# A planner's order changed: first loads, ranks, planned lengths, and one wide exponential in every third attention unit

## The chip, the cores and the metric

The kernel runs on one core of one Trainium2 chip. The metric is the time of one execution on the device in microseconds (us). The engines are TensorE (PE; its weight loads are listed as PEld), VectorE (DVE), ScalarE (ACT), GpSimd (POOL) and SyncE (SP), which only issues the transfers (DMAs) here.

## The reference

Banded attention feeds a gated feed-forward block with a spatial mixing. There are 8 batches, 8 heads, 576 positions and 64 features a head, all in float32 (w_in and w_out arrive as float64).

```python
scores = scale * np.matmul(q, k.transpose(0, 1, 3, 2))
mask_plain = (rel >= 0) & (rel < 32)                           # heads 0..3
mask_dil = (rel >= 0) & (rel < 128) & (rel % 4 == 0)           # heads 4..7
attn = softmax(np.where(masks, scores, -1e9))
x = np.matmul(attn, v)                                         # to (8, 576, 512)
h = np.maximum(x @ w_in, 0.0)                                  # 1024 wide
u, v = h[..., :512], h[..., 512:]
v_n = (v - mean(v)) / np.sqrt(var(v) + 1e-6)                   # over the 512 features
v_s = np.einsum('ts,bsd->btd', w_spatial, v_n) + b_spatial[None, :, None]
out = (u * v_s) @ w_out                                        # (8, 576, 512)
```

## The kernel before

**A planner writes the order.** The kernel is a set of strands, Python generators that yield what they need next (results of other strands, buffers, then an engine with a planned length in us) and emit their instructions when they are served. `Timeline.run` picks, again and again, the strand with the smallest `start + W * rank`: its planned start on its engine plus a small weight W times its rank. So each engine's instruction order, and SP's order of loads, is fixed when the kernel is built. On the chip an engine runs its instructions in that order and waits where an operand is late. The planned lengths steer only the choice; a rank of 1 is worth W us (0.12). `DVE2` and `POOL` share a planned port.

**Precision.** Matmuls with weights or features are made of three passes: each operand is split into a high and a low part (`h`, `l`), and high·high, high·low and low·high are added. The split of a float32 tile is a copy on ACT (line 348, 365, 578, 651 or 781, rounding to the high part) and a difference on DVE (`sub`, line 272) or POOL (`gsub`, line 275).

**Loads.** Everything loaded stands in 12 rotating buffers `kqv`. `heads_in` brings keys and queries of a pair of heads (4 pairs a batch), `values_in` its values, `weight_in` one of 8 chunks of w_in (`halves[half, c]`; half 1 is the value half, half 0 the gate's other factor) or 4 of w_out (`outs`), `spatial_in` one of 5 chunks of the spatial matrix, `bias_in` the bias. The list `first` is the order of the first loads on SP. Once the values of batch 0 and the first half of w_in are there, `reserve` takes nine of the buffers for good: three each for the sums of w_out (`o`), of w_in (`u`) and for `fac`.

**Weights.** `weight` turns a float64 chunk into high and low parts: ACT scales (line 311), DVE does four bit operations (313 to 321), ACT rounds the high part (348), and the low part is made in one of three ways, listed in `ways`: on PE as three matmuls with the identity and a copy by ACT (327 to 331), on DVE as two operations (272, 342), or on POOL. `spatial` splits a float32 chunk (ACT 365, DVE 272); it has a way over PE, which is switched off.

**Attention.** A unit is a third of the positions for two pairs of heads: 6 units a batch (two groups G, three units u each). Scores on PE (461), scale and mask (DVE 480), negated maximum (DVE 482), six exponentials with their sums on ACT (488), a small addition (ACT 491), reciprocal (DVE 501), the product with it on POOL (503), transposes on PE (508), a copy (ACT 511). `weighted` multiplies with the values (PE 536), `evacuated` copies to `raw` (ACT 563), `features_in` splits (ACT 578, DVE 272 and 582).

**Feed-forward.** `v_tile` makes 5 tiles of the value half (PE 605, 619), their rectified copy (ACT 611), statistics (DVE 637 to 639), the root on POOL (641) and the normalised, split tile (DVE 644, ACT 651; low part on POOL in batch 0 and on DVE after). `upper` is the other half for batch 0 (PE 681, ACT 686). From batch 1 on it is made with seven block products instead of eight (Strassen's scheme, `piece` with kind `u`, PE 818), which needs sums of blocks of w_in (`summed`, POOL 734 and 736, DVE, ACT) and factors, sums of feature blocks (`factor`, ACT 781 and DVE 272; `differences`, POOL 808). `gate` is the spatial mixing for a block of features and half of the positions (14 matmuls, PE 698 to 700) and the product with the other half on DVE (705). The output uses the same seven products (kind `o`); each product's result is added on DVE (854) or copied (ACT 856), and finished blocks go out (865). `warm` fills PE with matmuls on zeros (877) for the planned first 30 us.

Batch 1's attention is planned into batch 0's feed-forward, and so on; `AO` and `AS` set the ranks of its units.

Of the kernel before, what the change touches and what calls it, by code (L numbers as in the profile page):

```python
# [25 lines left out]
class Timeline:  # L26
# [71 lines left out]
    def run(self):  # L98
        W = 0.12
        while self.strands:  # L100
# [39 lines left out]
def tile_banded_attention_gated_moe(  # L140
# [24 lines left out]
    B, NPAIR, _, S = kT.shape  # L165
# [10 lines left out]
    US = 3  # L176
    NU = NS // US
# [179 lines left out]
    def spatial(sc):  # L357
        yield [("in", sc)]
        if sc == 4:
            yield [("bias",)]  # L360
        big = staged[sc]
        w = big[1][:, :S]
        yield ACT, 0.575, 0.1
        if sc < 4:
            nc.scalar.copy(wt[0][:, sc, :], w)
            if not (False):
                yield DVE2, 0.75
                sub(wt[1][:, sc, :], w, wt[0][:, sc, :])
            for ts in (slice(0, HS), slice(HS, S)) if False else ():
                yield "bank"  # L370
                (bank,) = yield PE, 0.63
                pl = bank[1][:, :HS]
                nc.tensor.matmul(pl, ident, w[:, ts], start=True, stop=False)
                nc.tensor.matmul(pl, minus, wt[0][:, sc, ts], start=False, stop=True)
                yield ACT, 0.29, 0.11
                nc.scalar.copy(wt[1][:, sc, ts], pl)
                tl.give(bank)
        else:
            nc.scalar.copy(wa, w)
            yield DVE2, 0.75  # L380
            sub(wb[:TAIL], w[:TAIL], wa[:TAIL])
        tl.give(big)
        tl.done("wt", sc)
# [63 lines left out]
    def unit(b, G, u):  # L447
# [34 lines left out]
        nc.vector.tensor_reduce(nm, flat, axis=AX.X, op=ALU.max, negate=True)  # L482
        if True:
            for e in range(US):
                yield ACT, 0.58 + 0.2 * (e == US - 1)
                for j in range(2):
                    i = 2 * e + j
                    nc.scalar.activation(  # L488
                        p[:, e, j], p[:, e, j], AF.Exp, bias=nm[:, i : i + 1], accum_out=sm[:, i : i + 1]
                    )  # L490
            nc.scalar.activation(sm, sm, AF.Copy, bias=1e-9)
            yield DVE, 0.11, 0.085
        else:
            yield POOL, 0.79, 0.04
            nc.gpsimd.tensor_add(flat, flat, nm.unsqueeze(2).broadcast_to([P, 2 * US, KW]))
            yield ACT, 0.425, 0.1
            nc.scalar.activation(p, p, AF.Exp)
            yield DVE, 0.83, 0.085
            nc.vector.reduce_sum(sm, flat, axis=AX.X)
            nc.vector.tensor_scalar_add(sm, sm, 1e-9)  # L500
# [56 lines left out]
    def evacuated(b, hp, h, acc):  # L557
        if hp >= NPAIR // 2:
            dst = raws[b, hp][1].rearrange("p (j r f) -> p f r j", f=2, r=2)[:, h]
        else:  # L560
            dst = raws[b, hp][1].rearrange("p (a r j) -> p a r j", a=2, r=2)[:, h]
        yield ACT, 0.3, 0.24
        nc.scalar.copy(dst, acc[1][1][:, :HS].rearrange("p (r j) -> p r j", r=2))  # L563
# [108 lines left out]
    def upper(b, h, f):  # L672
        fs = slice(f * P, (f + 1) * P)
        ts = slice(h * HS, h * HS + HS)
        yield [("v", b, t) for t in range(4)] + [("wi", 0, c) for c in range(NC)]
        yield "mm bank ur"
# [13 lines left out]
    def gate(b, h, f):  # L690
        fs = slice(f * P, (f + 1) * P)
        ts = slice(h * HS, h * HS + HS)
        yield [("vn", b, t) for t in range(5)] + [("wt", c) for c in range(5)] + [("bias",)]
        yield "mm bank"
        held = yield PE, 1.86
# [103 lines left out]
    def differences(b, kind, i):  # L799
# [5 lines left out]
        for n, need, a, c, to in zip((1, 3, 2, 4), needs, ((1, i), (1, 2 + i), (1, 2 + i), (0, i)), ((0, i), (1, i), (0, i), (0, 2 + i)), ((0, i), (1, i), (0, i), (0, 2 + i))):  # L805
            yield need
            yield POOL, 0.66, 0.04
            nc.gpsimd.tensor_sub(at(*to), at(*a), at(*c))  # L808
# [24 lines left out]
    def piece(b, kind, m, name, left, steps):  # L833

        if kind == "u" and len(name) == 2:
            yield [("v", b, t) for t in range(4)] + [("x", b, c, 0) for c in range(NC)]
        else:
            yield [("fac", b, kind, name)]
        yield [("wo", c) if kind == "o" else ("wi", 0, c) for c in range(NC)] + [("sum", kind, n, i) for n in range(1, 5) for i in range(2)]
        yield "mm bank"  # L840
        held = yield PE, 0.8
# [43 lines left out]

    ways = ((POOL, DVE, PE, DVE), (PE, PE, PE, PE), (PE, PE, DVE, DVE))
    halves = {}
    for half in (1, 0):
        cols = slice(half * NF, half * NF + NF)
        for c in range(NC):  # L890
# [3 lines left out]
            halves[half, c] = weight_in(("wi", half, c), src)  # L894
            r = -0.75 + 0.09 * c if half else -0.44 + 0.09 * c
            tl.add(r, weight(("wi", half, c), wi[0][:, c, cols], wi[1][:, c, cols], w_in.dtype, ways[1 - half][c]))
    outs = [weight_in(("wo", c), (w_out[c * P : c * P + P, 0],)) for c in range(NC)]
    first = [
        heads_in(0, 2), heads_in(0, 1, 0, 1), bias_in(), heads_in(0, 0, 0, 1), halves[1, 0], heads_in(0, 1, 1, NU),
        heads_in(0, 0, 1, NU), heads_in(0, 3), spatial_in(4), halves[1, 1], halves[1, 2], halves[0, 2],  # L900
        halves[0, 0], values_in(0, 0), values_in(0, 1), values_in(0, 2), halves[1, 3], halves[0, 3],
        values_in(0, 3), spatial_in(1), halves[0, 1], outs[2], outs[0], outs[3],
        outs[1], spatial_in(0), spatial_in(3), spatial_in(2),
    ]
    for n, strand in enumerate(first):
        tl.add(2 * n - 200, strand)
    for c in range(NC):
        tl.add(-1.06 + 0 * c, weight(("wo", c), wo[0][:, c, :], wo[1][:, c, :], w_out.dtype, ways[2][c]))
    for c in range(5):
        tl.add(-0.02 if c < 4 else -0.33, spatial(c))  # L910
    tl.add(-0.82, bias())
    for b in range(B):
        AO, AS = (-0.5, 0.4) if b == 1 else (0.1, 0.6)
        for hp in range(NPAIR):
# [11 lines left out]
        for n, (h, f) in enumerate(itertools.product(range(2), (0, 2, 1, 3))):  # L926
            if b < FU:
                tl.add(b + 0.15 + 0.02 * n, upper(b, h, f))
            tl.add(b + 0.3 + 0.05 * n, gate(b, h, f))
        for hp in range(NPAIR):  # L930
            tl.add(b - 1 + -0.25 + 0.01 * hp, features_in(b, hp))
        far = lambda row, col: lambda i: (col, 2 * row + i)
        for n, (name, source) in enumerate(
            (("11", far(0, 0)), ("21", far(1, 0)), ("1", far(0, 0)), ("2", far(0, 0)), ("3", far(0, 1)), ("22", far(1, 1)), ("4", far(1, 0)))
        ):
            tl.add(b + 1.0 + 0.0 * n, factor(b, "o", name, source))
            if b >= FU and len(name) == 1:
                tl.add(b + 0.1 + 0.0 * n, factor(b, "u", name, source))
        for i in range(2):
            tl.add(b + 1.0 + 0.01 * i, differences(b, "o", i))  # L940
            if b >= FU:
                tl.add(b + 0.7 + 0.01 * i, differences(b, "u", i))
        add, less = nc.vector.tensor_add, nc.vector.tensor_sub
        for kind, w_ in (("u", [x[:, :, :DM] for x in wi]), ("o", wo)):
# [9 lines left out]
            for m in range(2):  # L954
                for n, (name, left, steps) in enumerate(order):
                    r = b + (0.85 + 0.04 * n if kind == "o" else 0.3 + 0.02 * n) + 0.01 * m
                    if kind == "o" or b >= FU:
                        tl.add(r, piece(b, kind, m, name, left, steps))
    for n in range(3):
        tl.add(-0.75, reserve("o", n))  # L960
        tl.add(-0.75 + 0.01, reserve("u", n))
    for n in range(3):
        tl.add(-0.1, reserve("fac", n))
    for i in range(2):
        tl.add(0.0, summed("o", i))
        tl.add(0.8, summed("u", i))
    with tc.manual_schedule(engines={ENGINES.PE, ENGINES.Activation, ENGINES.DVE, ENGINES.Pool, ENGINES.SP}):
# [65 lines left out]
```

## Time and profile before

| | |
|---|---|
| median of 3 runs | 556.21 us (554.93 to 556.61) |
| the profiled execution | 554.37 us, its span 552.6 us |
| granted TensorE clock, mean | 0.989 |
| busy: PE, DVE, ACT, POOL | 538.2, 423.5, 331.9, 195.6 us |
| loaded and stored | 56.68 MB, mean 103 GB/s |

A row of a group of instructions reads: line, engine, operation, output<-input, shape, count | busy us, mean ns of one | idle time of the engine just before them, and what ended it. A row of the timeline is: start us, length us, engine, line, operation, count, and in brackets the idle time before it and what released it. A row of the table of stretches is: the stretch, its length, busy us of each engine (with the number of instructions), the granted clock, the busy share of the DMA engines, GB/s. The ends of PE's matmuls are modelled: its pace is read from the starts.

### The profile page before, as it was taken

What the parts mean: (1) busy time and instruction counts of PE and PEld (TensorE: products, weight loads), DVE (VectorE), ACT (ScalarE), POOL (GpSimd) and SP (SyncE); (2) the same over time, 40 slices, a digit from 0 to 9 for tenths busy, and PEclk for the clock granted to TensorE, in tenths of its full rate; (3) what the DMA queues carried; (4) which work ended last, traced back from release to release, by engine and by line L of the source; (5) the groups of instructions that cost most, each with busy time, mean ns of one, the idle gap of its engine ahead of it and who ended that gap; (6) DMA issues with size and microseconds to landing.
All of it is one profiled execution on the core that took longest, in us unless ns stands there. A gap on an engine that the chain in (4) does not pass through costs nothing.

```text
span 552.6 us, 18450 instructions
## 1 busy us (share of the span) xinstructions
PE 538.2 (97%) x7575; PEld 488.6 (88%) x7575; DVE 423.5 (77%) x1010; ACT 331.9 (60%) x1125; POOL 195.6 (35%) x239
## 2 busy tenths in 40 slices
PE   9899979999999999999999999999999999999997
PEld 7677769987899899998999899998999899998997
DVE  5688976899866795868866796868866796868846
ACT  4887688655738556574737556574737556574212
POOL 3310174643416241342416241342416241342231
PEclk9999997999999999999999999999999999999999
DMA  8996571200433414151433414161433414120102
GB/s 254 236 214 258 128 177 47 67 35 34 131 89 90 120 56 125 54 150 57 143 89 89 121 55 121 57 168 41 142 89 89 121 56 119 59 66 11 55 2 86
DMA packets 97449, 56.68 MB, mean 103 GB/s; under 512 B 78290, under 2 KB 87506, under 8 KB 97364
## 3 DMA queue, kind: packets, MB, share of 16 engines
q1 hardware_dynamic: 97364, 55.50, 36.1%
q8 instruction: 59, 0.97, 0.8%
q14 instruction: 26, 0.21, 0.1%
HBM read 46.04 MB, written 9.44 MB: 100 GB/s over the span
## 4 chain that ended last, share of the span: by engine, by line
PE 43%; DVE 25%; POOL 3%; ACT 3%; issue 1%; DVEq 0%; POOLq 0%
PE bank L818 17%; PE bank L698 13%; DVE fac L272 5%; DVE ur L854 4%; PE bank L536 4%; DVE bn L637 3%; PE bank L508 3%; DVE vnl L272 3%; PE bank L461 2%; PE bank L605 2%; ACT raw L563 2%; DVE nm L482 2%; DVE p L480 2%; DVE xl L272 2%; POOL p L503 2%; DVE mid L644 2%
## 5 line engine op out<-in xcount | busy, mean ns | idle before, releaser
L854 DVE TENSOR_TENSOR ur<-ur,bank 128x288 f32<-128x288 f32 x210 | 88.5, 447 | 34.3 <-PE bank L818 33.2
L488 ACT ACTIVATE p<-p,nm 128x64 f32<-128x64 f32 x288 | 96.2, 335 | 3.6 <-DVE nm L482 3.4
L781 ACT CAST fac<-ur 128x288 fp32r<-128x288 f32 x112 | 45.9, 434 | 74.8 <-DVE ur L705 52.9
L698 PE MATMUL bank<-wth,vnh 128*128 128x288 f32 x256 | 77.2, 302 | 0.0
L698 PE MATMUL bank<-wtl,vnh 128*128 128x288 f32 x256 | 75.7, 296 | 0.0
L698 PE MATMUL bank<-wth,vnl 128*128 128x288 f32 x256 | 75.6, 295 | 0.0
L641 POOL TENSOR_TENSOR rs<-rs,halfneg 128x1 f32<-128x1 f32 (+1 forms) x40 | 30.7, 768 | 121.5 <-DVE rs L639 121.5
L808 POOL TENSOR_TENSOR ur<-ur,ur 128x288 f32<-128x288 f32 x64 | 54.5, 856 | 48.9 <-DVE ur L705 39.6
L272 DVE TENSOR_TENSOR fac<-ur,fac 128x288 fp32r<-128x288 f32 x112 | 59.0, 540 | 7.7 <-ACT fac L781 6.9
L503 POOL TENSOR_TENSOR p<-p,rv 128x384 f32<-128x384 f32 x48 | 40.2, 843 | 53.0 <-DVE rv L501 42.0
L818 PE MATMUL bank<-fac,woh 128*128 128x288 f32 x256 | 54.1, 302 | 1.3 <-DVE ur L854 1.3
L488 ACT ACTIVATION_READ_ACCUMULATOR p<-p,nm 128x1 f32 x288 | 53.9, 187 | 0.0
L808 POOL TENSOR_TENSOR raw<-raw,raw 128x288 f32<-128x288 f32 x42 | 37.5, 900 | 46.2 <-DVE fac L272 26.0
L605 PE MATMUL bank<-wih,xl 128*128 128x512 f32 x128 | 50.1, 392 | 0.0
L605 PE MATMUL bank<-wih,xh 128*128 128x512 f32 x128 | 50.0, 391 | 0.0
L605 PE MATMUL bank<-wil,xh 128*128 128x512 f32 x128 | 49.9, 390 | 0.0
L698 PEld LDWEIGHTS bank<-wth,vnh 128*128 128x128 f32 x256 | 48.2, 188 | 0.6
L698 PEld LDWEIGHTS bank<-wtl,vnh 128*128 128x128 f32 x256 | 48.2, 188 | 0.0
L698 PEld LDWEIGHTS bank<-wth,vnl 128*128 128x128 f32 x256 | 48.1, 188 | 0.0
L705 DVE SCALAR_TENSOR_TENSOR ur<-ur,bank 128x288 f32<-128x288 f32 x64 | 28.7, 449 | 24.5 <-PE bank L700 23.7
L818 PE MATMUL bank<-fac,o 128*128 128x288 f32 x288 | 43.2, 298 | 0.0
L818 PEld LDWEIGHTS bank<-fac,woh 128*128 128x128 f32 x256 | 40.9, 189 | 2.3 <-DVE ur L854 1.8
(146 smaller groups left out, 1323.5 us busy)
## 6 DMA issues: line engine op xcount, KB each, us to landing
kqv<-in_vw_dram SPq DMA_DIRECT2D x128, 144.0 KB, 3.5
out_dram<-ur SPq DMA_DIRECT2D x64, 144.0 KB, 1.8
kqv<-in_kT_dram SPq DMA_DIRECT2D x30, 304.0 KB, 4.1
kqv<-in_qT_dram SPq DMA_DIRECT2D x30, 288.0 KB, 4.2
kqv<-in_w_in_dram SPq DMA_DIRECT2D x16, 256.0 KB, 6.4
kqv<-in_w_out_dram SPq DMA_DIRECT2D x4, 512.0 KB, 7.3
kqv<-in_w_spT_dram SPq DMA_DIRECT2D x5, 288.0 KB, 6.6
kqv<-in_kT_dram SPq DMA_DIRECT2D x2, 192.0 KB, 4.4
```

The source lines that it names most:

```text
L272: nc.vector.tensor_sub(out, a, b.bitcast(F32))
L488: nc.scalar.activation(p[:, e, j], p[:, e, j], AF.Exp, bias=nm[:, i : i + 1], accum_out=sm[:, i : i + 1])
L503: nc.gpsimd.tensor_mul(flat, flat, rv.unsqueeze(2).broadcast_to([P, 2 * US, KW]))
L536: nc.tensor.matmul(acc[j][1][1][i * D : i * D + D, (g - h * HB) * QB : (g - h * HB + 1) * QB], v[r, g, :], probs[b, G, u][1][r, e, q * QB ...
L605: nc.tensor.matmul(pm, x[c][a][:, cols], wi[w][:, c, NF:], start=c == 0 and n == 0, stop=c == NC - 1 and n == 2)
L641: nc.gpsimd.tensor_tensor(rs[:m], rs[:m], halfneg[:m], op=ALU.pow)
L698: nc.tensor.matmul(pv, vn[c][a][:, fs], wt[w][:, c, ts], start=n == 0, stop=False)
L705: nc.vector.scalar_tensor_tensor(ur, ur, 0.0, pv, op0=ALU.max, op1=ALU.mult)
L781: nc.scalar.copy(dst[:, 0, i, :], src)
L808: nc.gpsimd.tensor_sub(at(*to), at(*a), at(*c))
L818: nc.tensor.matmul(bank[:, :HS], left(i, w)[:, m * P : m * P + P], right, start=n == 0, stop=n == 5)
L854: op(ob[1], mine[src][1], bank[:, :HS])
```

## The change

Nothing of the arithmetic on batches changes but in the third unit of each group (`u == 2`). There POOL subtracts the maximum from the whole tile, ACT takes one exponential over all 384 columns, and DVE sums it and adds the small constant, in place of six exponentials with sums and ACT's addition. The code for it stood behind `if True` before:

```python
            yield POOL, 0.79, 0.04
            nc.gpsimd.tensor_add(flat, flat, nm.unsqueeze(2).broadcast_to([P, 2 * US, KW]))
            yield ACT, 0.425, 0.1
            nc.scalar.activation(p, p, AF.Exp)
            yield DVE, 0.83, 0.085
            nc.vector.reduce_sum(sm, flat, axis=AX.X)
            nc.vector.tensor_scalar_add(sm, sm, 1e-9)
```

The first loads come in another order, the low parts of weights are made in other ways (nine chunks over PE instead of seven, two over DVE instead of four, one over POOL as before), and two spatial chunks go over PE. The rest are planned lengths, ranks, W, and what a strand waits for in the plan.

```diff
     def run(self):
-        W = 0.12
+        W = 0.05
...
             nc.scalar.copy(wt[0][:, sc, :], w)
-            if not (False):
+            if not (sc in (1, 2,)):
...
                 sub(wt[1][:, sc, :], w, wt[0][:, sc, :])
-            for ts in (slice(0, HS), slice(HS, S)) if False else ():
+            for ts in (slice(0, HS), slice(HS, S)) if sc in (1, 2,) else ():
...
         nc.vector.tensor_reduce(nm, flat, axis=AX.X, op=ALU.max, negate=True)
-        if True:
+        if u < 2:
             for e in range(US):
-                yield ACT, 0.58 + 0.2 * (e == US - 1)
+                yield ACT, 0.664 + 0.115 * (e == US - 1), 0.1 * (e == US - 1)
...
             dst = raws[b, hp][1].rearrange("p (a r j) -> p a r j", a=2, r=2)[:, h]
-        yield ACT, 0.3, 0.24
+        yield ACT, 0.465 if hp >= NPAIR // 2 else 0.3, 0.1
...
         ts = slice(h * HS, h * HS + HS)
-        yield [("v", b, t) for t in range(4)] + [("wi", 0, c) for c in range(NC)]
+        yield [("v", b, t) for t in range(5)] + [("wi", 0, c) for c in range(NC)]
...
         yield [("vn", b, t) for t in range(5)] + [("wt", c) for c in range(5)] + [("bias",)]
+        if b >= FU:
+            yield [("prod", b, "u", (("21", "4"), ("22", "1"))[h][f // 2], f % 2)]
+        else:
+            yield [("used", b, h, f)]
...
             yield need
-            yield POOL, 0.66, 0.04
+            yield POOL, 0.77, 0.04
...
         if kind == "u" and len(name) == 2:
-            yield [("v", b, t) for t in range(4)] + [("x", b, c, 0) for c in range(NC)]
+            yield [("v", b, t) for t in range(5)] + [("x", b, c, 0) for c in range(NC)]
...
             yield [("fac", b, kind, name)]
+        if kind == "u":
+            yield [("made", b - 1, "o", n, "1w") for n in range(2)]
         yield [("wo", c) if kind == "o" else ("wi", 0, c) for c in range(NC)] + [("sum", kind, n, i) for n in range(1, 5) for i in range(2)]
+        chain = ("11", "21", "2", "3", "1", "22")
+        if name != "11":
+            yield [("prod", b, kind, chain[chain.index(name) - 1] if name in chain else "1", m)]
...
 
-    ways = ((POOL, DVE, PE, DVE), (PE, PE, PE, PE), (PE, PE, DVE, DVE))
+    ways = ((POOL, PE, PE, PE), (DVE, PE, PE, PE), (PE, PE, DVE, PE))
...
             halves[half, c] = weight_in(("wi", half, c), src)
-            r = -0.75 + 0.09 * c if half else -0.44 + 0.09 * c
+            r = -2.32 + 0.02 * c if half else -2.91 + 0.2 * c
...
     first = [
-        heads_in(0, 2), heads_in(0, 1, 0, 1), bias_in(), heads_in(0, 0, 0, 1), halves[1, 0], heads_in(0, 1, 1, NU),
-        heads_in(0, 0, 1, NU), heads_in(0, 3), spatial_in(4), halves[1, 1], halves[1, 2], halves[0, 2],
-        halves[0, 0], values_in(0, 0), values_in(0, 1), values_in(0, 2), halves[1, 3], halves[0, 3],
-        values_in(0, 3), spatial_in(1), halves[0, 1], outs[2], outs[0], outs[3],
-        outs[1], spatial_in(0), spatial_in(3), spatial_in(2),
+        halves[0, 0], heads_in(0, 0, 0, 1), heads_in(0, 1, 0, 1), halves[1, 0], heads_in(0, 2), bias_in(),
+        spatial_in(4), heads_in(0, 0, 1, NU), heads_in(0, 1, 1, NU), heads_in(0, 3), values_in(0, 0), halves[0, 3],
+        halves[1, 2], halves[0, 2], halves[1, 3], values_in(0, 1), outs[2], halves[1, 1],
+        values_in(0, 2), values_in(0, 3), spatial_in(1), halves[0, 1], outs[1], spatial_in(3),
+        outs[3], spatial_in(0), spatial_in(2), outs[0],
...
     for c in range(NC):
-        tl.add(-1.06 + 0 * c, weight(("wo", c), wo[0][:, c, :], wo[1][:, c, :], w_out.dtype, ways[2][c]))
+        tl.add(-1.01 + 0.24 * c, weight(("wo", c), wo[0][:, c, :], wo[1][:, c, :], w_out.dtype, ways[2][c]))
     for c in range(5):
-        tl.add(-0.02 if c < 4 else -0.33, spatial(c))
-    tl.add(-0.82, bias())
+        tl.add(0.57 if c < 4 else -1.09, spatial(c))
+    tl.add(-0.74, bias())
     for b in range(B):
-        AO, AS = (-0.5, 0.4) if b == 1 else (0.1, 0.6)
+        AO, AS = (-0.9, 0.7) if b == 1 else (0.1, 0.6)
...
             if b < FU:
-                tl.add(b + 0.15 + 0.02 * n, upper(b, h, f))
-            tl.add(b + 0.3 + 0.05 * n, gate(b, h, f))
+                tl.add(b + -0.6 + 0.06 * n, upper(b, h, f))
+            tl.add(b + 0.75 + 0.0 * n, gate(b, h, f))
         for hp in range(NPAIR):
-            tl.add(b - 1 + -0.25 + 0.01 * hp, features_in(b, hp))
+            tl.add(b - 1 + -0.2 + 0.01 * hp, features_in(b, hp))
...
         ):
-            tl.add(b + 1.0 + 0.0 * n, factor(b, "o", name, source))
+            tl.add(b + 0.95 + 0.0 * n, factor(b, "o", name, source))
             if b >= FU and len(name) == 1:
-                tl.add(b + 0.1 + 0.0 * n, factor(b, "u", name, source))
+                tl.add(b + 0.1 + 0.02 * n, factor(b, "u", name, source))
         for i in range(2):
-            tl.add(b + 1.0 + 0.01 * i, differences(b, "o", i))
+            tl.add(b + 0.95 + 0.01 * i, differences(b, "o", i))
             if b >= FU:
-                tl.add(b + 0.7 + 0.01 * i, differences(b, "u", i))
+                tl.add(b + 0.55 + 0.01 * i, differences(b, "u", i))
...
                 for n, (name, left, steps) in enumerate(order):
-                    r = b + (0.85 + 0.04 * n if kind == "o" else 0.3 + 0.02 * n) + 0.01 * m
+                    r = b + (0.85 + 0.03 * n if kind == "o" else 0.35 + 0.06 * n) + 0.01 * m
...
     for n in range(3):
-        tl.add(-0.75, reserve("o", n))
-        tl.add(-0.75 + 0.01, reserve("u", n))
+        tl.add(-0.7, reserve("o", n))
+        tl.add(-0.7 + 0.01, reserve("u", n))
     for n in range(3):
-        tl.add(-0.1, reserve("fac", n))
+        tl.add(0.95, reserve("fac", n))
     for i in range(2):
-        tl.add(0.0, summed("o", i))
-        tl.add(0.8, summed("u", i))
+        tl.add(0.5, summed("o", i))
+        tl.add(0.6, summed("u", i))
```

## The prediction

> **What bounds the kernel now.** I read the page's busy shares and slices first, since a planner's new order can only pay where the bounding engine has holes.
>
> ```profile
> span 552.6 us, 18450 instructions
> ...
> PE 538.2 (97%) x7575; PEld 488.6 (88%) x7575; DVE 423.5 (77%) x1010; ACT 331.9 (60%) x1125; POOL 195.6 (35%) x239
> ...
> PE   9899979999999999999999999999999999999997
> ...
> PEclk9999997999999999999999999999999999999999
> ```
>
> TensorE (PE) is busy for 97% of the span, and one slice, the seventh, shows a lower granted clock. The next view is the table of stretches, cut where the work changes: loading and first attention, first value tiles, the first batch's feed-forward, one regular batch, and the last batch.
>
> ```profile
> core 0: us, PE busy (x) PEld busy (x) DVE busy (x) ACT busy (x) POOL busy (x), PEclk, DMA share, GB/s
> 0.00:34.00 34.00, 31.21 (x396) 24.20 (x396) 20.97 (x56) 22.07 (x93) 12.21 (x25) 1.00 0.92 238
> 34.00:62.00 28.00, 27.77 (x380) 19.79 (x379) 24.46 (x48) 23.09 (x44) 0.69 (x1) 1.00 0.67 190
> 62.00:76.40 14.40, 13.95 (x229) 12.96 (x227) 13.88 (x33) 8.31 (x28) 6.83 (x7) 1.00 1.00 242
> 76.40:91.00 14.60, 11.24 (x271) 9.53 (x274) 7.65 (x19) 12.78 (x54) 8.17 (x9) 0.65 0.19 43
> 91.00:112.00 21.00, 21.00 (x327) 20.51 (x327) 18.12 (x37) 14.06 (x51) 12.21 (x11) 1.00 0.31 88
> 112.00:130.00 18.00, 18.00 (x132) 15.36 (x133) 17.45 (x46) 10.87 (x26) 8.96 (x10) 1.00 0.05 19
> 130.00:148.00 18.00, 16.36 (x217) 14.46 (x207) 17.00 (x42) 10.71 (x48) 7.36 (x9) 1.00 0.29 84
> ...
> 272.90:335.10 62.20, 61.96 (x932) 57.34 (x930) 47.59 (x117) 38.03 (x136) 22.41 (x29) 1.00 0.34 97
> 491.70:552.60 60.90, 57.24 (x390) 54.56 (x390) 44.69 (x104) 20.75 (x47) 15.70 (x19) 0.99 0.11 38
> ```
>
> A regular batch takes 62.2 us, of which PE idles 0.24: nothing to win there by order, something to lose. The holes lie elsewhere: 14.60 − 11.24 = 3.36 us at 76.4 to 91, where the clock is also 0.65; 1.64 us at 130 to 148, where VectorE (DVE) is busy for 17.00 of 18; and the warm-up time before 34. The hole at 76.4, instruction by instruction on PE:
>
> ```profile
> 76.27 0.29 PE L681 MATMUL bank<-xh,wil 128*128 128x288 f32 x1
> 78.00 0.55 PE L508 MATMUL bank<-plus,p 128*128 128x128 f32 x3 [1.45 <-POOL p L503]
> 79.70 0.55 PE L508 MATMUL bank<-plus,p 128*128 128x128 f32 x3 [1.16 <-POOL p L503]
> 81.00 2.25 PE L536 MATMUL bank<-pT,kqv 64*64 64x32 f32 x72 [0.75 <-ACT pT L511]
> ...
> 88.54 0.44 PE L681 MATMUL bank<-xl,wih 128*128 128x288 f32 x1
> 88.78 0.44 PE L681 MATMUL bank<-xh,wil 128*128 128x288 f32 x1
> ...
> 90.58 0.29 PE L681 MATMUL bank<-xl,wih 128*128 128x288 f32 x1
> 90.71 0.29 PE L681 MATMUL bank<-xh,wil 128*128 128x288 f32 x1
> ```
>
> The three waits sum to 3.36 us. After them equal matmuls start 0.24 us apart (88.54, 88.78) instead of 0.13 (90.58, 90.71): the clock is halved from 81.0 to about 90.4, which wastes half of 9.4 us, 4.7. **The hole costs 3.36 + 4.7 = 8.1 us of PE time.** Here a page speaks: the Trainium skill, "TensorE: Matmul & The Clock Gate", section "Why this matters for your kernels", asks for no PE-idle gaps over about 3 us, one idle window bringing the half clock. No single gap here exceeds 1.45 us, and the clock fell all the same; read gap by gap the rule would price the hole at 3.4 us and bring the forecast out 4.7 us later, about no change. The trace's clock speaks against that reading, so it gets no chance of its own: a cluster of short waits is enough.
>
> Who makes PE wait there is on GpSimd (POOL):
>
> ```profile
> 73.92 1.28 POOL L734 TENSOR_TENSOR mid<-woh,wol 128x512 f32<-128x512 f32 x1
> 75.17 1.29 POOL L736 TENSOR_TENSOR mid<-woh,wol 128x512 f32<-128x512 f32 x1
> ...
> 77.12 0.83 POOL L503 TENSOR_TENSOR p<-p,rv 128x384 f32<-128x384 f32 x1 [0.16 <-DVE rv L501]
> ...
> 81.93 2.50 POOL L275 TENSOR_TENSOR vnl<-mid,vnh 128x512 fp32r<-128x512 f32 x2
> ```
>
> Batch 1's attention and batch 0's normalised value tiles share POOL with the block sums (lines 734, 736), and the last value tile is done only at 84.4, because DVE was full (13.88 of 14.40) before. The gates need it; PE had nothing else left.
>
> **The change, part by part.**
>
> *More passes on PE.* PE finishes 9 weight chunks instead of 7 and two spatial chunks instead of none. Rows for the price, with the warm-up ahead of it:
>
> ```profile
> 24.93 7.55 PE L877 MATMUL bank<-vnl 128*128 128x512 f32 x32
> 32.31 1.06 PE L327 MATMUL bank<-kqv,plus 128*128 128x512 f32 x2
> ...
> 33.68 0.63 PE L877 MATMUL bank<-vnl 128*128 128x512 f32 x2
> ```
>
> One chunk holds PE from 32.31 to 33.68, 1.37 us; two more are 2.74. A spatial half has two of the three products and 288 of 512 columns: between 0.51 (scaled by both) and 0.77 us (by columns alone), taken 0.64, four of them 2.56. Together +5.3 us of PE work. But from 24.93 to 32.3 PE did nothing but 32 warm-up matmuls, and the new load order brings four chunks with a PE finish ahead of the second values load, where before one was finished by 34. Three more of them in warm-up time hide 3 × 1.37 = 4.1. Net **+1.2**; bounds −0.2 (a fourth hides as well) and +5.3 (none does, and the warm-up goes on as now). ScalarE (ACT) gets the extra copies, but loses more, below.
>
> *Less on DVE.* Ways that end on DVE fall from four to two, and two spatial differences go:
>
> ```profile
> 61.48 2.09 DVE L272 TENSOR_TENSOR wtl<-kqv,wth 128x576 fp32r<-128x576 f32 x3
> ...
> 65.74 0.69 DVE L272 TENSOR_TENSOR kqv<-kqv,woh 128x512 f32<-128x512 f32 x1
> 66.46 0.69 DVE L342 TENSOR_TENSOR wol<-kqv,mid 128x512 fp32r<-128x512 f32 x1
> ```
>
> That is 2 × 2 × 0.69 + 2 × 0.70 = 4.2 us less DVE before the value tiles are normalised.
>
> *Loads.* The loads run on one queue (SP's) in the listed order. Ahead of the second values load (pair 1) stood five w_in chunks, now six; ahead of the last values load (pair 3) one w_out chunk more than before. All else in front is the same.
>
> ```profile
> kqv<-in_w_in_dram SPq DMA_DIRECT2D x16, 256.0 KB, 6.4
> kqv<-in_w_out_dram SPq DMA_DIRECT2D x4, 512.0 KB, 7.3
> ```
>
> A w_in chunk is two transfers, 512 KB, as is a w_out chunk; at the 238 GB/s of the first stretch each is 2.2 us. So the first batch's attention outputs, and with them the value tiles, come up to **+2.2** later. Bounds 0 (PE hides it with chunks that it had to do anyway) and +4.4 (the chunk for features 1, now loaded behind pair 1's values and a w_out chunk, is late for the value tiles as well). I take 2.2, since both values loads are late by that.
>
> *The hole.* Three things work on it: 4.2 us less DVE ahead of the normalisation, weights processed before the attention is ready instead of at 50 to 67, and the block sums (ranks 0.0 to 0.5 and 0.8 to 0.6) and the spatial chunks (−0.02 to 0.57) ranked behind the value tiles at 0. The two sums of 1.28 and 1.29 us then no longer stand before the probabilities at 77.12, and the last value tile comes earlier than 84.4. On PE the first-batch upper products (62 to 76 now) still cover the normalisation. What is late next is the factors of the first output, which need the moved sums; the gates and the next value tiles stand between. I take 6.5 of 8.1 as recovered: one wait of about 1.5 us, as long as the longest here, stays. **−6.5**; bounds −8.1 and 0.
>
> *130 to 148.* PE loses 1.64 us there to a full DVE. The 4.2 us leave DVE earlier, the moved sums come nearer. **−1.0**; bounds −1.64 and +2 (the sums' DVE part no longer fits).
>
> *Third unit.* The lines view:
>
> ```profile
> L488 ACT ACTIVATE p<-p,nm 128x64 f32<-128x64 f32 x288 | 96.2, 335 | 3.6 <-DVE nm L482 3.4
> ...
> L503 POOL TENSOR_TENSOR p<-p,rv 128x384 f32<-128x384 f32 x48 | 40.2, 843 | 53.0 <-DVE rv L501 42.0 <-DMA kqv<-in_w_spT_dram 8.0 <-PE bank L508 1.7
> ...
> L482 DVE TENSOR_REDUCE nm<-p 128x6 f32<-128x384 f32 x48 | 26.6, 553 | 1.6
> ...
> L511 ACT COPY pT<-bank 128x384 f32<-128x384 f32 x48 | 22.4, 480 | 9.7 <-PE bank L508 9.3
> ...
> L491 ACT ACTIVATE sm<-sm 128x6 f32<-128x6 f32 x48 | 10.0, 208 | 1.5
> ```
>
> Six exponentials (6 × 0.335) and the small copy (0.21) make 2.2 us of ACT; one wide one is priced by the equally large copy, 0.48. So 16 units lose 1.7 us each on ACT. They gain a subtraction of 0.84 on POOL and a sum of 0.55 and a small addition (about 0.2, the row of line 491) on DVE. Latency: 2.2 + 0.84 before, 0.84 + 0.48 + 0.75 + 0.84 = 2.9 after, the same within 0.2. In a regular batch two such units leave DVE at 47.6 + 1.5 and POOL at 22.4 + 1.7 of 62.2: covered, **0**. Without the cover, with the unit's two POOL steps behind other POOL work, each could cost PE one wait of 0.75 to 1.45 us as in the hole.
>
> *New orderings in every batch* (products in a fixed chain, second-half products behind the previous output's sixth sum, gates behind their product, W 0.05): no instruction more, **0**, bounds −0.24 and +1.1 us in each of seven batches, that is −1.7 and +7.7; the upper end is rival 1. *Buffers for factors reserved later* free three of twelve load buffers for batch 1's loads, 0 in the sum since the queue idles at 76.4 to 91 (DMA share 0.19). *The tail* after the last matmuls is the same chain: 0, ±1.
>
> **Sum:** 1.2 + 2.2 − 6.5 − 1.0 = −4.1. The profiled execution took 554.37 us (span 552.6 and 1.8 around it), 1.8 less than the median of 556.21; the sum goes to the median: 552.1, predicted 552.0.
>
> **Rivals.**
> 1. *The gates are no longer filler (slower).* Today gates run between second-half products while the factors for those are made on ACT and DVE. When a gate must wait for its product, any late factor stops PE, with everything queued behind it in program order. Against it: DVE has 14.6 us free per batch. For it: PE has only 0.24 us. At 1.1 us a batch, seven batches are +7.7: 559.8. From 0.6 us a batch it eats the gain. Chance 0.18.
> 2. *The hole moves forward.* The value tiles' second input chunk of weights arrives after pair 1's values; if PE runs dry there for 3.4 us in short waits, the clock halves again: +8.1, 560. For it: the load order; against: four PE chunks can fill. Chance 0.12.
> 3. *DVE takes the place of PE.* From 91 to 148 DVE is busy for 52.6 of 57 us; closing the hole pushes the same DVE work into less time, and PE waits there instead. The gain is returned: 555.5. Chance 0.14. It is also the case in which the new order does nothing.
> 4. *All of it works:* hole gone (−8.1), 130 to 148 closed (−1.64), load delay hidden (0), passes hidden (−0.2): −9.9, 546.3. Chance 0.12.
>
> The forecast itself has 0.44, its own range 549.5 to 554.5.
>
> **How the numbers follow.** A measurement of this kernel tells about 0.3% (1.7 us) from no change. Faster by more: the forecast but for its upper edge (0.42), rival 4 (0.12), part of rival 3 (0.04): 0.58. Within: the rest of rival 3 (0.10), the forecast's edge (0.02), mild forms of rivals 1 and 2 (0.07): 0.19. Slower: the rest of rivals 1 and 2, 0.23. The range reaches from rival 4, 546.0, to rival 1, 559.8.
>
> **What would show it.** Right: granted clock 1.00 in every stretch after 30 us; no wait of PE on line 503 over 1 us between 70 and 90; PE chunk finishes (line 327) before 30 us; the last value tile's difference before 80; regular batches at 62.2. Wrong: a batch period over 62.8 with PE waiting ahead of line 818; a clock below 1 between 36 and 50; DVE over 97% from 90 to 140 with PE waits on line 854.

## The result, and the profile after

The changed kernel took 560.07 us (median of seven runs, 558.06 to 561.89) against 556.42 us of the kernel before on the same chip: a ratio of 1.0064, 95% interval 1.0037 to 1.0091. It is slower by 0.6%, where 552.0 had been forecast, and lies just outside the range. The profiled execution took 560.05 us. One of the seven runs had a granted clock of 1.000 and took 558.06 us, the others had 0.993 to 0.997.

The page of the changed kernel, busy shares, slices and the chain that ended last:

```profile
span 558.2 us, 18325 instructions
...
PE 539.1 (97%) x7594; PEld 491.6 (88%) x7594; DVE 430.6 (77%) x1036; ACT 308.5 (55%) x939; POOL 206.7 (37%) x255
...
PE   9999999999999999989999899999999999999997
...
PEclk9999999999999998999999999999999999999999
...
PE 78%; DVE 10%; ACT 4%; DMA 4%; issue 2%; POOL 1%; SPq 0%; DVEq 0%; ACTq 0%; POOLq 0%
```

At this grain the page is no worse than before: the slow slice in the loading stage is gone, PE is at 97%. Yet "DMA 4%" now stands in the chain. The table of stretches, cut as in the prediction, with one stretch added (210 to 218):

```profile
core 0: us, PE busy (x) PEld busy (x) DVE busy (x) ACT busy (x) POOL busy (x), PEclk, DMA share, GB/s
0.00:34.00 34.00, 31.37 (x395) 24.23 (x396) 21.80 (x59) 18.83 (x68) 12.75 (x26) 1.00 0.95 233
34.00:62.00 28.00, 26.64 (x373) 19.09 (x372) 23.86 (x49) 23.73 (x46) 2.46 (x3) 1.00 1.00 255
62.00:76.40 14.40, 13.18 (x209) 10.80 (x207) 11.31 (x28) 11.11 (x40) 10.04 (x12) 1.00 0.28 72
76.40:91.00 14.60, 14.60 (x319) 13.79 (x320) 13.29 (x23) 9.62 (x25) 9.84 (x8) 1.00 0.46 100
91.00:112.00 21.00, 20.52 (x315) 19.07 (x314) 19.80 (x47) 14.27 (x51) 8.96 (x10) 1.00 0.31 88
...
130.00:148.00 18.00, 17.57 (x305) 16.43 (x307) 16.61 (x44) 11.95 (x44) 8.27 (x10) 1.00 0.32 94
210.00:218.00 8.00, 6.63 (x166) 6.29 (x165) 3.07 (x9) 4.04 (x10) 0.00 (x0) 0.79 0.21 46
272.90:335.10 62.20, 60.08 (x918) 55.82 (x917) 47.50 (x116) 33.50 (x102) 21.97 (x28) 1.00 0.33 91
```

The hole at 76.4 to 91 is closed: PE 14.60 of 14.60 at clock 1.00. One wait of its kind is left, just ahead of that stretch:

```profile
76.37 0.55 PE L508 MATMUL bank<-plus,p 128*128 128x128 f32 x3 [1.22 <-POOL p L503]
```

A regular batch, which had 0.24 us of idle PE before, now has 2.12. So the loading stage did what was hoped, and the place held to be neutral lost.

The length of a batch says the same. I read it from the timeline of PE as the time from one batch's first gate (the first weight load of line 699 before, 703 after) to the next one's. "Gates of batch 2" is the moment when the loading stage and the first two batches are over.

| kernel | gates of batch 2, us | batches 2 to 6, us | from batch 7's gates to the end of the span, us |
|---|---|---|---|
| before | 204.8 | 62.5 62.2 62.2 62.1 61.6 | 37.1 |
| after | 204.0 | 66.7 64.0 63.2 63.5 59.4 | 37.4 |
| store first (below) | 203.0 | 62.8 61.6 61.6 61.6 59.3 | 37.5 |

Which wait is it? The list of waits has two rows that the kernel before hasn't (columns: who waits, for whom: total us, count, longest):

```profile
DVE ur L863 <- DMA out_dram<-ur: 7.9, 4, 2.5
PE bank L822 <- DVE fac L272: 7.1, 5, 2.1
```

Four waits of DVE on an output store, and PE behind them on the factors. Instruction by instruction in batch 3, first DVE and then PE:

```profile
305.75 0.82 DVE L863 TENSOR_TENSOR ur<-ur,bank 128x288 f32<-128x288 f32 x2
306.56 1.31 DVE L272 TENSOR_TENSOR xl<-raw,xh 128x576 fp32r<-128x576 f32 x1
...
312.55 1.18 DVE L863 TENSOR_TENSOR ur<-ur,bank 128x288 f32<-128x288 f32 x3 [2.47 <-DMA out_dram<-ur]
313.65 0.82 DVE L272 TENSOR_TENSOR fac<-ur,fac 128x288 fp32r<-128x288 f32 x2
```

```profile
311.34 0.69 PE L822 MATMUL bank<-fac,o 128*128 128x288 f32 x4
314.16 0.53 PE L822 MATMUL bank<-fac,o 128*128 128x288 f32 x2 [2.12 <-DVE fac L272]
```

An addition of line 863 makes an output tile and ends at 306.57. Its store isn't issued until 309.37, as SP's queue shows. First the changed kernel, then the kernel before (start, us held on the queue, transfers):

```profile
305.47 0.34 SPq L874 DMA_DIRECT2D out_dram<-ur  x1
305.87 3.40 SPq L443 DMA_DIRECT2D kqv<-in_vw_dram  x4
309.37 0.57 SPq L874 DMA_DIRECT2D out_dram<-ur  x1
```

```profile
303.98 1.79 SPq L865 DMA_DIRECT2D out_dram<-ur  x2
305.87 2.57 SPq L443 DMA_DIRECT2D kqv<-in_vw_dram  x4
```

Before: both stores, then the four transfers of a values load. After: store, load, store. Issuing the load holds SP for 3.40 us, so the second store goes out 2.8 us after its tile is ready. The next addition wants that `ur` buffer and waits 2.47 us, its factor is late, and PE stops for 2.12 us.

### The profile page after: what moved, and what is told of

It is laid out like the page before. It is cut to its first block, busy times and chain, and to the rows that moved or that the text cites. A ratio compares the mean times of both kernels' runs of the same rounds, so it can differ in the third digit from the quotient of the medians.

```text
span 558.2 us, 18325 instructions
## 1 busy us (share of the span) xinstructions
PE 539.1 (97%) x7594; PEld 491.6 (88%) x7594; DVE 430.6 (77%) x1036; ACT 308.5 (55%) x939; POOL 206.7 (37%) x255
## 4 chain that ended last, share of the span: by engine, by line
PE 78%; DVE 10%; ACT 4%; DMA 4%; issue 2%; POOL 1%; SPq 0%; DVEq 0%; ACTq 0%; POOLq 0%
PE bank L822 27%; PE bank L702 17%; PE bank L605 14%; PE bank L536 6%; PE bank L461 4%; PE bank L508 3%; DMA out_dram<-ur 2%; ACT p L488 2%; DVE ur L863 2%; PE bank L681 1%; PE bank L886 1%; PE bank L704 1%; PE bank L703 1%; DVE xl L272 1%; PE bank L619 1%
## 5 line engine op out<-in xcount | busy, mean ns | idle before, releaser
L272 DVE TENSOR_TENSOR fac<-ur,fac 128x288 fp32r<-128x288 f32 x112 | 55.0, 508 | 26.6 <-ACT fac L785 26.4
L488 ACT ACTIVATE p<-p,nm 128x64 f32<-128x64 f32 x192 | 64.1, 336 | 7.1 <-DVE nm L482 6.5
L812 POOL TENSOR_TENSOR raw<-raw,raw 128x288 f32<-128x288 f32 x42 | 34.3, 824 | 72.1 <-DVE fac L272 61.3
L822 PE MATMUL bank<-fac,o 128*128 128x288 f32 x288 | 45.3, 299 | 7.1 <-DVE fac L272 7.1
L822 PEld LDWEIGHTS bank<-fac,o 128*128 128x128 f32 x288 | 40.8, 188 | 10.1 <-DVE fac L272 8.4
L536 PEld LDWEIGHTS bank<-pT,kqv 64*64 64x64 f32 x2304 | 36.7, 135 | 7.5 <-issue 5.8
```

Source lines behind the costliest of these rows:

```text
L272: nc.vector.tensor_sub(out, a, b.bitcast(F32))
L488: nc.scalar.activation(p[:, e, j], p[:, e, j], AF.Exp, bias=nm[:, i : i + 1], accum_out=sm[:, i : i + 1])
L536: nc.tensor.matmul(acc[j][1][1][i * D : i * D + D, (g - h * HB) * QB : (g - h * HB + 1) * QB], v[r, g, :], probs[b, G, u][1][r, e, q * QB ...
L822: nc.tensor.matmul(bank[:, :HS], left(i, w)[:, m * P : m * P + P], right, start=n == 0, stop=n == 5)
```

## The experiments

**Theory A**: the second store behind the values load is the loss; take it away and the change is the gain that was forecast, or more. **Rival B**: the loss is the wide exponential, through POOL and DVE. **Rival C**: it is the new order of gates and second-half products itself (the prediction's rival 1). **Rival D**: the loading stage loses elsewhere what it won at the hole. The runs come from three rounds, in which the kernel before took 557.35 us (e1 to e4), 556.28 (e5 to e8) and 556.72 (e9 to e12), so a difference of about 1 us between rounds says nothing; the ratios are to the kernel before of the same round.

**1. Store first (e1_store_first).** The values load that falls between two stores is issued right behind the second. All other engines' orders stay as they are in the changed kernel.

```
+        if stores[b - 2] == 1:
+            behind.append(issue)      # the four dma_start of the load
+        else:
+            issue()
...
                 nc.sync.dma_start(out[b, ...], ob[1])
+                stores[b] += 1
+                while behind:
+                    behind.pop()()
```

> The changed kernel with one thing moved: on SP, from batch 2 on, the values load that stands between the first two output stores of the previous batch is issued right behind the second store. The orders of PE, DVE, ACT and POOL stay exactly those of the changed kernel. Theory A (a store that queues behind a values load on SP frees its ur buffer late, DVE waits for that buffer, PE waits for DVE): the waits of DVE on the output store (7.9 us in four batches) go, a regular batch falls from 63.2-64.0 to 62.2-62.6 us, the time from 560.1 to 552.5-555. Rival B (the new orderings of products and gates take PE's filler away, rival 1 of the prediction): the batch stays above 63 us, the time 559-561.

Measured: 549.38 us (548.47 to 552.32), ratio to the kernel before 0.9867 (0.984 to 0.9894). That is 10.7 us less than the changed kernel, from the place of four transfers in one queue. SP, then DVE, then the stretch of one batch:

```profile
300.56 1.81 SPq L882 DMA_DIRECT2D out_dram<-ur  x2
302.48 2.57 SPq L446 DMA_DIRECT2D kqv<-in_vw_dram  x4
```

```profile
305.10 1.17 DVE L871 TENSOR_TENSOR ur<-ur,bank 128x288 f32<-128x288 f32 x3
```

```profile
265.80:327.40 61.60, 61.60 (x932) 57.59 (x931) 48.98 (x122) 34.90 (x111) 23.84 (x29) 1.00 0.36 99
```

The three additions no longer wait, and PE is busy for 61.60 of 61.60 us. A holds, and is worth more than I expected; B and C can't be the loss, since nothing of either was undone: DVE, ScalarE and POOL run the same instructions in the same order as in the changed kernel.

**2. The reverse (e2_reverse).** In the kernel before, the second store of batches 1 to 5 is held until the values load has been issued.

```
+                stores[b] += 1
+                if 1 <= b < B - 2 and stores[b] == 2:
+                    behind.append(lambda: nc.sync.dma_start(place, ob[1]))
+                else:
+                    nc.sync.dma_start(place, ob[1])
...
+        while behind:             # in values_in, behind the load
+            behind.pop()()
```

> The kernel before with the same thing done to it the other way: the second output store of a batch is issued behind the values load that followed it. All other orders stay those of before. Theory A: DVE waits on an output store in each regular batch, the batch grows from 62.2 to 63-64 us, the time from 556.4 to 558.5-563. Rival B: 556.4 within 1, since no product or gate moves. If ur is not needed as soon in this order, A expects less than 1 us and the trace shows no wait of DVE on a store.

Measured: 561.76 us (559.30 to 564.66), ratio 1.0094 (1.0061 to 1.0128). The old kernel loses from the same cause, but less: in the profiled execution batches 1 to 6 take 3.7 us more in all than before, and batches 2 to 5 62.7 to 63.4 us each, where I had expected 63 to 64. Another 1.2 us came ahead of the first gates of batch 1, before any store that was moved. Its row in the list of waits:

```profile
DVE ur L857 <- DMA out_dram<-ur: 4.0, 5, 1.1
```

**3. Issue time or landing? (e9_store_by_act).** In the changed kernel the second store goes out by ScalarE's queue, so it overtakes the load's issue but shares the DMA engines with it.

```
-                nc.sync.dma_start(out[b, ...], ob[1])
+                stores[b] += 1
+                queue = nc.scalar if stores[b] == 2 else nc.sync
+                queue.dma_start(out[b, ...], ob[1])
```

> The changed kernel with the second output store of each batch issued by ScalarE's queue, at its place in the plan; the values load stays first on SP, and both still share the 16 DMA engines. If the delay is SP's issue of four transfers (2.6 us): the store starts at once, DVE's wait on it falls under 0.5 us a batch, 550-552. If it is the transfers' share of the DMA engines (the store lands in 3.5 us instead of 1.8): DVE still waits 1 us or more a batch, 554-558. ScalarE pays at most the issue itself.

Measured: 550.69 us, ratio 0.9891 (0.9867 to 0.9915), and DVE no longer waits on a store. The DMA issues (columns: count, KB each, median us from issue to landing):

```profile
out_dram<-ur SPq DMA_DIRECT2D x56, 144.0 KB, 1.8
out_dram<-ur ACTq DMA_DIRECT2D x8, 144.0 KB, 2.1
```

The four stores that go out beside a load, in batches 2 to 5, landed after 1.9 to 2.4 us. In the changed kernel the four that were queued behind one landed after 2.9 to 3.5. So in batch 3 the late store lost 2.8 us to SP's queue and another 1.3 on its way (3.1 against the median of 1.8). How much the slower landing would cost without the late issue was not tested. The Trainium skill, "Trainium Kernel Development and Optimization", section "Key Constraints", says that the queues of SP, ScalarE and GpSimd feed the same 16 DMA engines, so a second issuer adds no bandwidth and saves only issue time. These rows agree: the store from the second queue wins by going out earlier, and doesn't land faster.

**4. The planner told the truth (e10_longer_store).** The planner gives a store's buffer back 2.5 us after issue; here 6.0.

```
-                tl.now += 2.5
+                tl.now += 6.0
```

> The changed kernel with the planned time of an output store until its buffer is free set to 6.0 us instead of 2.5, nothing else; SP's order keeps the store behind the values load. Theory A, and the planner able to use it: other work is put ahead of the addition that needs the buffer, DVE does not wait on the store, 549.5-553. If the ten ur buffers leave no other order: PE still waits, 556-560.

Measured: 551.04 us, ratio 0.9896 (0.9872 to 0.992). SP's order is still store, load, store, but DVE doesn't wait on a store any more. So a late store by itself costs nothing here; it costs when its buffer is taken up again too early. The order of DVE's additions and differences changed too, so the run doesn't tell whether another order or another buffer took the wait away.

**5. The third unit (e3_narrow, e7_wide_first_two, e8_wide_later, e12_wide_alone).** The first puts six narrow exponentials back everywhere in the changed kernel, the next two start from experiment 1 and keep the wide one in part, the last puts the wide one into the kernel before (there together with the chain of products, as the planner finds no order without it).

```
-        if u < 2:                 # after: units 0 and 1 narrow, the third wide
+        if True:                  # e3: all narrow
+        if u < 2 or b >= 2:       # e7: wide in batches 0 and 1 alone
+        if u < 2 or b < 2:        # e8: wide from batch 2 on
```

```
-        if True:                  # e12, in the kernel before
+        if u < 2:
...
+        chain = ("11", "21", "2", "3", "1", "22")
+        if name != "11":
+            yield [("prod", b, kind, chain[chain.index(name) - 1] if name in chain else "1", m)]
```

> The changed kernel with six narrow exponentials in the third unit, as before. The plan it gives has both stores ahead of the values load. Theory A: the slow batch is gone as in the run with the store moved, 552.5-556, and the wide exponential is worth nothing by itself (within 1.5 us of that run). Rival C (the wide exponential's POOL and DVE work delays the factors): clearly less than the run with the store moved, by 2 us or more. Rival B: 559-561.

Measured: 560.84 us, ratio 1.0072 (1.0048 to 1.0096). No gain, and my expectation failed, for a reason that the times of the gates show: all narrow, the planner put both stores ahead of the load in regular batches (61.9 us each), but the gates of batch 2 came at 214.8, 10.8 us later than in the changed kernel. Two effects of one edit had cancelled, so I separated them.

> The kernel with the store moved (e1), with the wide exponential only in batches 0 and 1 and six narrow ones from batch 2 on. Prediction's price (worth nothing in a regular batch): 549.4 within 1, regular batches at 61.6-61.9 us. If it is worth something there: 551-553, batches over 62.

> The kernel with the store moved (e1), with six narrow exponentials in batches 0 and 1 and the wide one from batch 2 on. If the wide exponential's worth lies in the loading stage, where ScalarE is busy for up to 9 of 10 us: the first gates of batch 0 come later by 5-13 us, and the time is 555-561. If it lies in neither: 549.4 within 1.

Measured: 548.69 us (548.12 to 549.91), ratio 0.988 (0.9851 to 0.9909), with the wide exponential in the first two batches alone; 563.65 us, ratio 1.0143 (1.0114 to 1.0171), with it everywhere but there. In the second a hole is back: PE is busy for 12.28 of 14.40 us, and then the clock is at 0.60:

```profile
62.00:76.40 14.40, 12.28 (x217) 8.52 (x219) 12.36 (x33) 11.30 (x49) 5.48 (x8) 0.93 0.03 5
76.40:91.00 14.60, 13.74 (x246) 12.65 (x242) 6.33 (x11) 8.07 (x20) 9.98 (x9) 0.60 0.64 164
```

The first of the two has the lowest median here, but by the ratios it can't be told from experiment 1 (0.988 and 0.9867). From batch 2 on the form of the exponential makes no difference that these runs show. In the loading stage, with these loads and ranks and the order that the planner makes of them, the wide one is worth 14.3 us (563.65 against 549.38).

> The kernel before with the wide exponential in every third unit, and the fixed chain of products (without which the planner finds no order); loads, ways and ranks as before. Both stores stand ahead of the values load. If the wide exponential helps by itself in the loading stage: 549-554, first gates of batch 0 before 93. If its worth comes only with the new ranks: 556 within 2, or slower where the ranks no longer fit.

Measured: 561.97 us, ratio 1.0096 (1.007 to 1.0121). In the old loading stage the same edit, with the chain, loses: the first gates of batch 0 come at 94.7, not before 93, and those of batch 1 at 151.6 instead of 140.8. So "wide is good" is no rule. B is ruled out by experiment 1, which keeps the wide exponential and is rid of the loss all the same. That it pays where ScalarE is late is my reading; no run shows it.

**6. The loading stage in parts (e4_prologue_alone, e5_ways_back, e6_first_back).** e4 puts the new first loads, ways and ranks into the kernel before. e5 and e6 start from experiment 1: the old ways (with spatial chunks 1 and 2 by differences on DVE), and the old list of first loads.

```
-    ways = ((POOL, PE, PE, PE), (DVE, PE, PE, PE), (PE, PE, DVE, PE))      # e5
+    ways = ((POOL, DVE, PE, DVE), (PE, PE, PE, PE), (PE, PE, DVE, DVE))
...
-        halves[0, 0], heads_in(0, 0, 0, 1), heads_in(0, 1, 0, 1), ...      # e6
+        heads_in(0, 2), heads_in(0, 1, 0, 1), bias_in(), ...
```

> The kernel before with the new first loads, ways, ranks of weights, spatial chunks and bias, and the two spatial chunks over PE; batches as before. By the traces' balance up to 148 us (8.0 us less lost on PE, 5.3 us more work, nothing hidden) 2.7 us less: 553-554.5. By the prediction's sum 4.1 less: 552. If the prologue's gain is lost on the way into the regular batches (both kernels start batch 1's gates at 140.8): 556 within 1.

Measured: 553.79 us (552.25 to 557.93), ratio 0.995 (0.9928 to 0.9973): the new loading stage alone is a gain of 0.5%, as expected. The profiled execution took 556.64 us, and in it the gates of batch 2 come 1 us later than before, so the trace doesn't show where the gain lies.

> The kernel with the store moved (e1), with the old ways of making low parts: seven chunks over PE, four over DVE, both spatial chunks on DVE. Theory P (PE pays for every added pass, none hides in the warm-up): 5.3 us less PE work in the first 90 us, 544-547 against 549.4. Theory D (DVE is what the gates of batch 0 wait for, the passes were well spent): 4.2 us of DVE come back before the normalised tiles, the hole or a later first gate with them: 549-556.

Measured: 555.69 us, ratio 0.999 (0.9969 to 1.0011), 6.3 us more than experiment 1. DVE has more to do in the first of these stretches (25.88 us against 24.50), and PE runs out of work:

```profile
34.00:62.00 28.00, 23.60 (x346) 15.34 (x346) 25.88 (x49) 21.14 (x41) 2.94 (x4) 0.88 0.97 258
...
76.40:91.00 14.60, 14.60 (x304) 14.06 (x303) 11.32 (x26) 8.97 (x22) 7.49 (x8) 0.81 0.39 95
```

> The kernel with the store moved (e1), with the old order of the first loads and everything else new. If the new load order cost what the trace suggests (value tiles end 6.3 us later than before), the value tiles end earlier again and the time falls by 2-5 us: 544.5-547.5. If it is what lets the weights through and closed the hole: slower, 551-558, with a PE wait or a half clock between 70 and 95.

Measured: 556.79 us (552.67 to 560.42), ratio 1.0014 (0.998 to 1.0048), 7.4 us more than experiment 1; the runs spread widely. The loads, the ways and the wide exponential are each worth 6 to 14 us *given the other two*; their sum far exceeds the 1.8 us by which experiment 1's gates of batch 2 lead the kernel before. In each of these runs the planner also wrote another order, so the numbers aren't prices of the parts: they were planned together and aren't separable. D isn't the loss, since the gates of batch 2 come 0.8 us earlier than before; but most of what the hole gave was spent ahead of them.

**7. The weight W (e11_w012).** W from 0.05 to 0.12 in the changed kernel.

```
-        W = 0.05
+        W = 0.12
```

> The changed kernel with W at 0.12 as before. Its plan has both stores ahead of the values load. Theory A: regular batches at 61.6-62.2 us. The loading stage is another order too: if it holds its gain, 549-553; if the loading stage depends on W as it does on its other parts, 555-561 with a clock under 0.9 between 40 and 91.

Measured: 557.46 us, ratio 1.0016 (0.9997 to 1.0036). Batches 3 to 5 fall to 61.6 to 62.0 us, since the planner happens to order the stores otherwise, but the loading stage is worse (first gates of batch 0 at 102.1 instead of 91.3).

## Why the prediction was wrong

The step that failed is **New orderings in every batch**, put at 0 with bounds of −1.7 and +7.7 us. It considered PE, DVE and POOL and left out SP's queue, though in the new order a load moves past a store there. By the table the changed kernel's profiled execution is about 5.7 us longer: 0.8 less up to the gates of batch 2 (forecast −4.1), 6.2 more in batches 2 to 6 (forecast 0), 0.3 more behind. The orders of the other engines are a gain, as experiment 1 shows: 61.6 us instead of 62.2 a batch. Moving the store took 10.7 us away (560.07 − 549.38), 9.8 of them in batches 2 to 5 by the table above (66.7 + 64.0 + 63.2 + 63.5 less 62.8 and three times 61.6). In batch 2 that includes a stretch of half clock: PE idle for 1.37 us at 210 to 218 and the clock at 0.79 there; experiment 1 has a gap of 0.94 us at the same instructions, at full clock. The longer gap and the clock (0.21 of 8.00 us) make 2.1 us; that they come from the store is not shown. The other 7.7 are near the 7.1 us that PE waited on factors. Rival 1 named nearly the measured time, 559.8, by another mechanism: gates that wait for products. PE did wait on late factors, as it said, but the factors were late because of a store, and with the gates' order untouched experiment 1 is one of the fastest kernels here. So its number is no success.

The other steps:

- *More passes on PE* (+1.2): the saving was wrong. I let 4.1 of 5.3 us hide in the warm-up. The first chunk's finish (line 327) comes at 32.87, where it was 32.31 before, and the warm-up matmuls (now line 886) run on until then, so none hid, and the term stands at its upper bound of +5.3:

```profile
28.88 4.15 PE L886 MATMUL bank<-vnl 128*128 128x512 f32 x17
32.87 1.06 PE L327 MATMUL bank<-kqv,plus 128*128 128x512 f32 x2
```

- *Loads* (+2.2): too small. The last value tile's matmuls of batch 0 (line 619) begin at 63.2 instead of 56.9, 6.3 us later; the weights that PE finished meanwhile filled most of it, as idle PE at 34 to 76.4 grew only from 0.68 to 2.58 us, with the 1.22 of the wait that stayed among them.
- *The hole* (−6.5): right, in size too. The clock stays at 1.00, and of the waits one stayed, 1.22 us where I had taken about 1.5, so −6.9. It ends at 76.37, just ahead of the stretch in the table, which is why that shows none.
- *130 to 148* (−1.0): PE 17.57 instead of 16.36, so −1.2. Right.
- These together were forecast at −4.1. The gates of batch 2 come 0.8 us earlier than before in the changed kernel and 1.8 in experiment 1 (a rough measure, since the gates have other ranks now); the passes and loads took most of the hole's gain back. That the sum of 552.0 is near experiment 1's 549.4 rests partly on gains of the new orderings that I had put at 0.
- *Third unit* (0): right from batch 2 on, wrong as a statement on the loading stage, where it carries the closed hole. The prices were near (columns: count, busy us, mean ns, idle before):

```profile
L495 POOL TENSOR_TENSOR p<-p,nm 128x384 f32<-128x384 f32 x16 | 14.8, 924 | 3.8 <-DVE nm L482 2.8 <-DVE rv L501 0.8
L497 ACT ACTIVATE p<-p 128x384 f32<-128x384 f32 x16 | 8.4, 524 | 4.5 <-POOL p L495 4.5
L499 DVE TENSOR_REDUCE sm<-p 128x6 f32<-128x384 f32 x16 | 8.7, 545 | 1.9 <-ACT p L497 1.8
L500 DVE TENSOR_SCALAR sm<-sm 128x6 f32<-128x6 f32 x16 | 5.5, 346 | 0.6
```

  Forecast were 0.84, 0.48, 0.55 and 0.2.
- Rival 2 (the hole moves forward) shows at 34 to 76.4 at most as the 2.58 us above, at full clock. Rival 3 (DVE takes PE's place) did not come: DVE is at 19.80 of 21.00 at 91 to 112, and PE idles 0.48.

Of the signs that I had named, "a batch period over 62.8 with PE waiting ahead of line 818" (now 822) came true. Of the signs of being right, the clock of 1.00 after 30 us failed at one place, 210 to 218; the chunk finishes came at 32.87 and not before 30; the wait of 1.22 us on line 503 stayed; and the last value tile's difference on POOL ends at 80.5 instead of before 80. The range's lower end, 546.0, should have been the 546.3 of rival 4.

What stays open: why PE idled 1.37 us in the attention of batch 2 (the profile names no releaser, only "issue", and between 213 and 214 us no other engine works either), whether that gap and its half clock hang on the store, and how the three parts of the loading stage depend on each other beyond what their removal shows.

## What to carry to other kernels

When an order changes, write down every queue that issues transfers too, store by store: a store whose buffer is soon taken up again must not stand behind a load that takes microseconds to issue. A planner that counts a store as done a fixed time after its own step doesn't see the queue ahead of it; either give it the queue's time or order stores ahead of loads by hand. And before judging a bundle of edits by its total, look for one wait that is new in the list of waits: here one of up to 2.5 us, four times, hid a gain of 1.3%.

## What the hardware showed that I had not expected

Issuing is slow enough to matter: four transfers of 144 KB took 2.57 to 3.40 us of SP's queue in the rows above, more than the 1.8 us in which a store of 144 KB lands. And the small addition of line 500, 128 x 6, took 0.35 us on average, about as much as a narrow exponential of 128 x 64 (0.34), with single ones from 0.17 to 0.60; I didn't find out why.
